# Weight block sums moved from GpSimd additions to accumulating DMAs, with three raw buffers in turn, in a kernel of attention and two expert layers

## The chip, the cores and the metric

One core of a Trainium2 chip runs the whole program in one launch. The metric is the device time in microseconds (us), median of several runs. Lower is better.

## The reference

Attention is computed for 2 batches, 8 heads, 768 positions and head size 64: a local window and 24 block summaries per head. Its output, 1536 tokens of 512 values, goes through two dense expert layers. All is float32.

```python
def _moe_ref(x, domain_probs, w1, w2):          # 4 experts, 512 -> 1024 -> 512
    p = domain_probs / (domain_probs.sum(-1, keepdims=True) + 1e-09)
    for e in range(E):
        h = np.maximum(x @ w1[e], 0.0)
        out += p[:, e:e + 1] * (h @ w2[e])
def _moe2_ref(x, w_gate, w1, w2):               # 8 experts
    P = np.exp(logits - logits.max())           # logits = x @ w_gate
    for _ in range(8):
        P /= P.sum(1, keepdims=True) + 1e-09
        P /= P.sum(0, keepdims=True) + 1e-09
        P *= N / E
    for e in range(E):
        out += P[:, e:e + 1] * (np.maximum(x @ w1[e], 0.0) @ w2[e])
```

## The kernel before

**Units and steps.** The two layers have 12 experts with 1024 hidden columns each. A unit is 256 hidden columns of one expert, so there are 48 units: 16 in the first layer, 32 in the second. The tokens form two blocks of 768. A step is one unit with one block: 96 steps. The border is the last step of the first layer, step 31.

**Seven products.** Both multiplications of a step are done on 2x2 blocks by a Strassen scheme of Winograd's form, with seven products instead of eight. The weights give the left operands: three raw blocks (`A11`, `A12`, `A22`) and four sums of blocks (`S1` to `S4`). The activations give the right operands: three raw blocks (`B11`, `B21`, `B22`) and four differences (`T1` to `T4`). Every operand is split into a high and a low float32r part (`hi`, `lo`), and three matmuls of 128x384 make one product of a 128 deep slice. A first product (`product`, L509, on `w1`) is six matmuls; a second product (L760, on `w2`) is three, and there are two rows of seven of them. A step is thus 42 + 42 matmuls.

**Weights (`add_weights`).** SP loads four raw 256-column blocks of `w1` or `w2` into a buffer `raw` (L641); each kind has one buffer of its own. ScalarE writes `hi` (L648) and the negated raw block into `lo` (L649). Then GpSimd issues a DMA that adds the raw block onto it (L652), which leaves the low part. This is done for a group of three raw blocks, then GpSimd forms the four sums in place with four `TENSOR_TENSOR` instructions (L659, `sums_of`), then two groups of two sums follow. The places for the raw-block groups are double, those for the sums are single: a new sum goes in only after the last matmul of the unit before has read the old one.

**Between the two multiplications.** ScalarE copies the first bank into others (`fork`, L684) so that products can accumulate; VectorE adds, applies ReLU times the row of expert weights (`relu`, L523), and forms the operands of the second multiplication (`add_hop`: `hi` on ScalarE L729, `lo` on VectorE L629). The second products are added to accumulators by VectorE (`evac`) or copied by ScalarE.

**The turn (`add_turn`).** At the border the accumulators of the first layer become the operands of the second: per block and half, seven additions on VectorE, seven `hi` on ScalarE, seven `lo`, of which VectorE makes four and GpSimd three. `add_gate` multiplies with `w_gate` on TensorE, `add_sinkhorn` does the eight normalisations in small VectorE instructions, and `plain` says in which units of the second layer's first expert ReLU is applied without the row, since it isn't there yet: all four. `add_scale` multiplies it in afterwards.

**The order.** All this is entered with `op` as a list of work with an engine, a cost (`SPAN`), its reads and writes and a due time. `run_work` plays the list through and writes each engine's instructions in the order that comes out. On the chip every engine and DMA queue runs its own list in that order. `FIRST`, `SECOND`, `HOP`, `GOFF`, `DCOFF`, `LEAD` and `LEAD2` set the due times.

Of the kernel before, what the change touches and what calls it, by code (L numbers as in the profile page):

```python
# [18 lines left out]
def local_global_attention_moe_moe(  # L19
# [92 lines left out]
    raw = {k: xp.tile([P, 4, FU], F32, name=f"raw{k}") for k in (1, 2)}  # L112
    quad = {n: xp.tile([P, HB], F32, name=n) for n in ("q11", "q12", "q21", "q22", "t2", "t4")}
# [4 lines left out]
    NU = len(units)  # L118
    KEYS = ("m1", "m2", "z", "c12", "c22")
# [20 lines left out]
    def loads(kind, u):  # L140
        layer, e, f = units[u]
        r = raw[kind]
        f0, f1, f2 = f * FU, f * FU + P, (f + 1) * FU
        if kind == 1:
            w = (w1a, w1b)[layer][e]
            h = DM // 2

            def part(c0, c1, a, z):
                return w[c0:c1, a:z].rearrange("(c p) f -> p c f", p=P)

            return [
                (r[:, 1:3].rearrange("x b (c f) -> x (b c) f", f=P), part(0, DM, f0, f1), (1, 2)),
                (r[:, 0].rearrange("x (c f) -> x c f", f=P), part(h, DM, f1, f2), (0,)),
                (r[:, 3].rearrange("x (c f) -> x c f", f=P), part(0, h, f1, f2), (3,)),
            ]
# [11 lines left out]
    def sums_of(kind):  # L167
        r = raw[kind]
        return (
            (0, ALU.add, 3, 0),  # L170
            (3, ALU.subtract, 1, 3),
            (1, ALU.subtract, 0, 1),
            (2, ALU.subtract, 2, 1),
        )

    def w_pieces(u, kind, hi_eng, lo_eng, sum_eng):
        r = raw[kind]
        hi, lo = wop[kind]
# [348 lines left out]

    def products(S, px, py, pz):
# [15 lines left out]
        vadd(q22, px, q22)  # L544
# [6 lines left out]
        product(S, A22, T4, px, False)  # L551
        relu(S, q21, px, 0)
# [74 lines left out]
    def lo_op(eng, out, src, hi, reads, writes, due, n=1):  # L627
        def fn(e=nc.gpsimd if eng == "POOL" else nc.vector):
            e.tensor_tensor(out=out, in0=src, in1=hi.bitcast(F32), op=ALU.subtract)  # L629

        span = ("p384", "p768")[n - 1] if eng == "POOL" else ("v", "v768")[n - 1]
        op(eng, span, reads, writes, due, fn, True)

    def add_weights(u, kind, start):
        r = raw[kind]
        hi, lo = wop[kind]
        R = [("raw", kind, i) for i in range(4)]
        for o, i, blocks in loads(kind, u):
            op(
                "SP", "ld", (), [R[x] for x in blocks], start,  # L640
                lambda o=o, i=i: nc.sync.dma_start(out=o, in_=i),  # L641
            )

        def group(s, n, b, key, due, span):
            src = r[:, b:b + n]
            h, l = hi[:, s:s + n], lo[:, s:s + n]
            rd = R[b:b + n]
# [3 lines left out]
                "POOL", "pd", rd, [key + ("lo",)], due + 0.05,  # L651
# [3 lines left out]
        group(slot(u, A22), 3, 0, wkey(kind, u, A22), start + 0.2, "a768")  # L655
        for o, f, x, y in sums_of(kind):
# [578 lines left out]
```

## Time and profile before

| | us |
|---|---|
| median of 3 runs (1613.19 to 1619.2) | 1614.82 |
| the profiled execution's own time | 1613.51 |
| its span in the profile | 1611.8 |
| TensorE busy in the span | 1541.8 (96%) |
| VectorE busy | 1393.4 (86%) |
| ScalarE busy | 1195.9 (74%) |
| GpSimd busy | 636.2 (39%) |

The span runs from the first to the last instruction of one execution. Busy TensorE time is not the same as full speed: matmuls overlap, and the clock that was granted is told apart in its own column. What counts is where TensorE sits idle, at which clock it runs, and whom it waits for.

### The profile page before, as it was taken

The page shows a single profiled execution, that of the slowest core. Times are in us where ns is not written, and L with a number is a line of the kernel's source. Part 1 is how long each engine was busy: PE and PEld are TensorE (multiplying, and loading weights), DVE is VectorE, ACT ScalarE, POOL GpSimd, SP SyncE. Part 2 cuts the span into 40 slices and gives each one's busy share as a digit, 9 for nine tenths or more (in the row PEclk, how much of TensorE's full clock was granted, in tenths as well). Part 3 has the DMA queues.
Part 4 walks back from the last instruction along what each step waited for, and adds up shares of the span by engine and source line. Part 5 has one row for each costly group of instructions (what it writes and reads, how often), then busy time and mean ns, then how long its engine had stood idle before and what let it go on. Part 6 is the DMA issues. An engine that isn't in the chain of part 4 may idle for free.

```text
span 1611.8 us, 26658 instructions
## 1 busy us (share of the span) xinstructions
PE 1541.8 (96%) x9098; PEld 1495.8 (93%) x9098; DVE 1393.4 (86%) x2694; ACT 1195.9 (74%) x2566; POOL 636.2 (39%) x753
## 2 busy tenths in 40 slices
PE   7888999999999988999999999999999999999998
PEld 6778999999999986998899999999999999999997
DVE  6877879988889997799998998888988988888988
ACT  5768777777778775866786877777776877777775
POOL 2864334334344344233333434334333433344330
PEclk9999999999999997999999999999999999999999
DMA  7823554554554542354354455544544554544542
GB/s 173 208 64 79 106 114 87 107 112 89 106 122 90 112 88 43 69 117 102 80 114 108 96 108 112 105 102 101 110 98 102 105 102 102 108 102 105 108 79 92
DMA packets 169241, 166.36 MB, mean 103 GB/s; under 512 B 44032, under 2 KB 128400, under 8 KB 169104
## 3 DMA queue, kind: packets, MB, share of 16 engines
q0 software_dynamic: 40608, 86.26, 30.9%
q1 hardware_dynamic: 128496, 78.39, 16.8%
q8 instruction: 71, 1.16, 0.3%
q14 instruction: 66, 0.54, 0.1%
HBM read 73.97 MB, written 3.22 MB: 48 GB/s over the span
## 4 chain that ended last, share of the span: by engine, by line
PE 61%; DVE 13%; DMA 12%; ACT 4%; issue 2%; POOL 0%; SPq 0%; ACTq 0%; DVEq 0%; POOLq 0%
PE bank L760 30%; PE bank L509 30%; DMA raw<-in_moe_w_dram 6%; DMA w1lo<-raw 5%; DVE h L629 4%; DVE q L523 2%; DVE t L133 1%; DVE z L130 1%; DVE c L130 1%; DMA w2lo<-raw 1%; DVE q L133 1%; DVE m L130 1%; ACT q L684 1%; ACT w1hi L648 1%; DVE q L130 1%
## 5 line engine op out<-in xcount | busy, mean ns | idle before, releaser
L760 PE MATMUL bank<-h,w2hi 128*128 128x384 f32 x2688 | 693.9, 338 | 13.0 <-ACT bank L771 4.6
L760 PEld LDWEIGHTS bank<-h,w2hi 128*128 128x128 f32 x2688 | 485.6, 189 | 26.9 <-DVE h L629 10.3
L509 PE MATMUL bank<-xhi,w1hi 128*128 128x384 f32 x1330 | 451.7, 340 | 19.3 <-ACT q L684 12.3
L509 PE MATMUL bank<-xhi,w1lo 128*128 128x384 f32 x1330 | 448.3, 337 | 2.5 <-DMA w1lo<-raw 2.5
L760 PE MATMUL bank<-h,w2lo 128*128 128x384 f32 x1344 | 450.6, 335 | 0.0
L509 PE MATMUL bank<-xlo,w1hi 128*128 128x384 f32 x1330 | 448.6, 337 | 2.0 <-DVE xlo L629 1.2
L659 POOL TENSOR_TENSOR raw<-raw 128x256 f32<-128x256 f32 x376 | 329.2, 876 | 298.3 <-issue 147.7
L629 DVE TENSOR_TENSOR h<-q,h 128x384 fp32r<-128x384 f32 x480 | 284.6, 603 | 9.2 <-ACT h L729 7.5
L771 ACT COPY bank<-bank 128x384 f32<-128x384 f32 x384 | 181.0, 471 | 143.3 <-PE bank L760 139.2
L509 PEld LDWEIGHTS bank<-xhi,w1hi 128*128 128x128 f32 x1330 | 251.9, 189 | 28.2 <-ACT q L684 19.1
L729 ACT CAST h<-q 128x384 fp32r<-128x384 f32 x480 | 241.9, 514 | 38.4 <-DVE q L133 19.6
L509 PEld LDWEIGHTS bank<-xlo,w1hi 128*128 128x128 f32 x1330 | 252.1, 190 | 3.9 <-DVE xlo L629 2.8
L509 PEld LDWEIGHTS bank<-xhi,w1lo 128*128 128x128 f32 x1330 | 252.1, 190 | 3.8 <-DMA w1lo<-raw 3.8
L760 PEld LDWEIGHTS bank<-h,w2lo 128*128 128x128 f32 x1344 | 253.4, 189 | 0.1
L652 POOL DMA_DIRECT2D w1lo<-raw x141 | 122.1, 866 | 317.9 <-PE bank L760 166.7
L652 POOL DMA_DIRECT2D w2lo<-raw x141 | 122.7, 870 | 254.5 <-ACT w2lo L649 158.3
L130 DVE TENSOR_TENSOR c<-bank,c 128x384 f32<-128x384 f32 x368 | 196.6, 551 | 4.7 <-PE bank L760 3.3
L130 DVE TENSOR_TENSOR q<-bank,q 128x384 f32<-128x384 f32 x190 | 105.3, 554 | 84.5 <-PE bank L509 81.7
L648 ACT CAST w1hi<-raw 128x768 fp32r<-128x768 f32 x141 | 97.9, 694 | 66.8 <-DMA raw<-in_moe_w_dram 42.5
L523 DVE SCALAR_TENSOR_TENSOR q<-bank,pb 128x384 f32<-128x384 f32 x174 | 96.3, 553 | 51.4 <-PE bank L509 47.4
L629 DVE TENSOR_TENSOR h<-t,h 128x384 fp32r<-128x384 f32 x192 | 120.8, 640 | 11.3 <-ACT h L729 10.4
L771 ACT COPY m<-bank 128x384 f32<-128x384 f32 x192 | 92.3, 481 | 41.1 <-PE bank L760 39.1
(177 smaller groups left out, 1809.9 us busy)
## 6 DMA issues: line engine op xcount, KB each, us to landing
raw<-in_moe_w_dram SPq DMA_DIRECT2D x96, 256.0 KB, 3.2
raw<-in_moe_w_dram SPq DMA_DIRECT2D x192, 128.0 KB, 3.1
w1lo<-raw POOLq DMA_DIRECT2D x94, 256.0 KB, 4.0
w2lo<-raw POOLq DMA_DIRECT2D x94, 256.0 KB, 3.3
w1lo<-raw POOLq DMA_DIRECT2D x47, 384.0 KB, 3.8
w2lo<-raw POOLq DMA_DIRECT2D x47, 384.0 KB, 4.8
pb<-prow SPq DMA_DIRECT2D x22, 384.0 KB, 3.8
vs<-in_v_dram SPq DMA_DIRECT2D x16, 240.0 KB, 4.3
```

The lines of the kernel that those rows point to most:

```text
L130: (eng or nc.vector).tensor_tensor(out=out, in0=x, in1=y, op=ALU.add)
L133: (eng or nc.vector).tensor_tensor(out=out, in0=x, in1=y, op=ALU.subtract)
L509: nc.tensor.matmul(pm, l[:, s, cs_], r[:, x, :], start=first and i == 0, stop=i == n - 1, skip_group_check=True,)
L523: nc.vector.scalar_tensor_tensor(out=out, in0=src, scalar=0.0, in1=PB[S[1]][:, th * HB:(th + 1) * HB], op0=ALU.max, op1=ALU.mult,)
L629: e.tensor_tensor(out=out, in0=src, in1=hi.bitcast(F32), op=ALU.subtract)
L648: aop(lambda: nc.scalar.copy(out=h, in_=src), rd, [key + ("hi",)], due, span)
L652: lambda: nc.gpsimd.dma_start(out=l, in_=src, accum_op=ALU.add),
L659: lambda o=o, f=f, x=x, y=y: nc.gpsimd.tensor_tensor(out=r[:, o], in0=r[:, x], in1=r[:, y], op=f),
L684: aop(lambda: nc.scalar.copy(out=out, in_=src), [kin], [kout], due)
L729: aop(lambda: nc.scalar.copy(out=hi, in_=q[name]), [name], [("hi", i)], due, "ah")
L760: nc.tensor.matmul(cut[bank], l[:, s, cols], hop[t][:, r], start=start and i == 0, stop=i == 2, skip_group_check=True,)
L771: aop(lambda: nc.scalar.copy(out=out, in_=src), [kin], [kout], due)
```

## The change

The sign variant: the `T` operands are renamed `N` and partly negated, so that every weight sum is an addition in place, in three operations of two, one and two blocks. GpSimd no longer adds them; it issues a DMA from raw block to raw block that accumulates. There are three raw buffers (the third is the attention's last output tile `xf`), used in turn by both kinds. The low parts of the turn and of `add_x` go to VectorE entirely. The rows of the second layer go into `PB`, plain units are three (`NPL`), and the planner's costs, product orders and due times have other values. The second gate half has 16 matmuls instead of 12. In attention, the first unit's sums are still made by GpSimd, in three instructions per kind, and VectorE negates one operand per x tile.

```diff
-    SLOT = {A22: 0, A11: 1, A12: 2, S1: 6, S2: 7, S4: 8, S3: 9}
+    SLOT = {A12: 0, A22: 1, A11: 2, S1: 6, S2: 7, S4: 8, S3: 9}
...
-    raw = {k: xp.tile([P, 4, FU], F32, name=f"raw{k}") for k in (1, 2)}
+    raws = [xp.tile([P, 4, FU], F32, name=f"raw{k}") for k in (1, 2)]
+
+    def turn_of(kind, u):
+        return (2 * (u - 1) + kind - 1) % 3 if u else kind - 1
...
-    def sums_of(kind):
-        r = raw[kind]
+    def sums_of(kind, u):
+        r = raw_of(kind, u)
         return (
-            (0, ALU.add, 3, 0),
-            (3, ALU.subtract, 1, 3),
-            (1, ALU.subtract, 0, 1),
-            (2, ALU.subtract, 2, 1),
-        )
+            (r[:, 0:2], r[:, 2:4], (0, 1), (2, 3)),
+            (r[:, 3], r[:, 2], (3,), (2,)),
+            (r[:, 0:3:2], r[:, 1:2].to_broadcast([P, 2, FU]), (0, 2), (1,)),
+        )
...
     def plain(S):
         layer, e, f = units[S[0]]
-        return layer == 1 and e == 0
+        return layer == 1 and e == 0 and f < NPL
...
-        "pd": (0.87, 4.2), "ld": (0.06, 3.2), "st": (0.06, 2.2),
+        "add1": (0.87, 4.0),
+        "add2": (0.87, 4.8), "add3": (0.87, 5.5), "ld": (0.06, 4.3), "st": (0.06, 2.2),
...
-        group(slot(u, A22), 3, 0, wkey(kind, u, A22), start + 0.2, "a768")
-        for o, f, x, y in sums_of(kind):
+        group(slot(u, A12), raws[i][:, 0:3], (0, 1, 2), wkey(kind, u, A12), start + 0.2, "a768")
+        for o, x, wr, rd in sums_of(kind, u):
             op(
-                "POOL", "p256", [R[x], R[y]], [R[o]], start + 0.5,
-                lambda o=o, f=f, x=x, y=y: nc.gpsimd.tensor_tensor(
-                    out=r[:, o], in0=r[:, x], in1=r[:, y], op=f
-                ),
-                True,
-            )
-        group(6, 2, 0, wkey(kind, u, S1), start + LEAD2, "a512")
-        group(8, 2, 2, wkey(kind, u, S4), start + LEAD2 + 0.1, "a512")
+                "POOL", f"add{len(wr)}", [R[j] for j in (*rd, *wr)], [R[j] for j in wr], start + 0.5,
+                lambda o=o, x=x: nc.gpsimd.dma_start(out=o, in_=x, accum_op=ALU.add),
+            )
+        group(6, *pair_of(kind, u, 0), wkey(kind, u, S1), start + LEAD2, "a512")
+        group(8, *pair_of(kind, u, 1), wkey(kind, u, S4), start + LEAD2 + 0.1, "a512")
...
-        for th, ops in ((0, ((B11, 0), (B21, 1))), (1, ((B11, 0), (T1, 0), (B22, 1)))):
+        for th, ops in ((0, ((B11, 0), (B21, 1))), (1, ((B11, 0), (N2, 0), (B22, 0), (B22, 1)))):
...
-    FIRST = {0: "1567324", 1: "1567342"}
-    SECOND = {0: "1256437", 1: "1524637"}
-    HOP, GOFF, DCOFF, LEAD, LEAD2 = 1.13, 0.16, 4.0, 1.0, 1.11
+    FIRST = {0: "1562734", 1: "1567342"}
+    SECOND = {0: "1526473", 1: "1526437"}
+    HOP, GOFF, DCOFF, LEAD, LEAD2 = 1.04, 0.16, 4.4, 1.0, 1.09
     LOPOOL = ()
+    LATER = {-2: 1.0, 1: -0.4, 2: -0.2, 3: 0.8}
+    SOONER = {-2: 0.6, -1: 0.2, 0: 0.2, 1: 0.6, 2: 1.0, 3: -0.2}
+    TURN = 0.8
```

**The order on GpSimd in the second layer.** Each engine runs its rows one after the other. Here is about one unit on GpSimd before; `raw_91` holds `w1`, `raw_92` holds `w2`, "waits" names semaphores of ScalarE, TensorE, SP's loads (`DMAHW`) and GpSimd's own DMAs (`DMASW`).

```order
L659 TENSOR_TENSOR raw_92<-raw_92 128x256 [waits DMASW4_49,Pool_49]
L659 TENSOR_TENSOR raw_92<-raw_92 128x256 [waits Pool_49] x2
L652 DMA w1lo<-raw_91 128x768 [waits DMAHW4_49,DMAHW7_49,PE_49,Activation_49]
L659 TENSOR_TENSOR raw_91<-raw_91 128x256 [waits DMAHW0_49,DMASW5_49,DMASW0_49]
L652 DMA w2lo<-raw_92 128x512 [waits PE_49,Activation_49]
L659 TENSOR_TENSOR raw_91<-raw_91 128x256 [waits DMASW7_49,Pool_49]
L659 TENSOR_TENSOR raw_91<-raw_91 128x256 [waits Pool_49]
L652 DMA w2lo<-raw_92 128x512 [waits Activation_49]
L659 TENSOR_TENSOR raw_91<-raw_91 128x256 [waits Pool_49]
L652 DMA w1lo<-raw_91 128x512 [waits PE_49,Activation_49]
L652 DMA w1lo<-raw_91 128x512 [waits PE_49,Activation_49,Pool_49]
L652 DMA w2lo<-raw_92 128x768 [waits DMAHW3_49,DMAHW2_49,Activation_49]
```

And one unit on GpSimd with the change; the twelve rows repeat with the three buffers in turn.

```order
L690 DMA raw_92<-raw_92 128x512 [waits DMASW4_49]
L690 DMA raw_92<-raw_92 128x256 [waits DMASW7_49]
L683 DMA w1lo<-xf 128x768 [waits DMAHW4_49,DMAHW5_49,DMASW1_49,DMAHW6_49,PE_49,Activation_49]
L690 DMA raw_92<-raw_92 128x2x256 [waits DMASW2_49,DMASW0_49]
L690 DMA xf<-xf 128x512 [waits DMAHW7_49,DMASW1_49]
L690 DMA xf<-xf 128x256 [waits DMASW3_49]
L683 DMA w2lo<-raw_92 128x512 [waits DMASW2_49,DMASW5_49,PE_49,Activation_49]
L683 DMA w2lo<-raw_92 128x2x256 [waits DMASW6_49,Activation_49]
L690 DMA xf<-xf 128x2x256 [waits DMASW4_49]
L683 DMA w2lo<-raw_91 128x768 [waits DMAHW1_49,DMAHW0_49,Activation_49]
L683 DMA w1lo<-xf 128x512 [waits DMASW7_49,PE_49,Activation_49]
L683 DMA w1lo<-xf 128x2x256 [waits Activation_49]
```

Each sum is now a DMA that waits for the landing of the sum before it, and the DMAs that make low parts stand between them on the same queue.

**The order on VectorE and GpSimd at the turn.** Before, GpSimd makes six of the first block's fourteen low parts (`xlo`).

```order
L629 TENSOR_TENSOR xlo_82<-c_00_1575,xhi_81 128x384
L652 DMA w2lo<-raw_92 128x768
L629 TENSOR_TENSOR xlo_82<-c_00_1577,xhi_81 128x384
L629 TENSOR_TENSOR xlo_82<-m_00_1571,xhi_81 128x384
L629 TENSOR_TENSOR xlo_84<-c_01_1576,xhi_83 128x384
L652 DMA w1lo<-raw_91 128x768
L629 TENSOR_TENSOR xlo_84<-c_01_1578,xhi_83 128x384
L629 TENSOR_TENSOR xlo_84<-m_01_1572,xhi_83 128x384
```

With the change all fourteen are on VectorE, between its other work; this is the densest piece.

```order
L652 SCALAR_TENSOR_TENSOR xlo_84<-z_1574,xhi_83 128x384
L657 TENSOR_TENSOR xlo_84<-c_01_1576,xhi_83 128x384
L144 TENSOR_TENSOR m_10_1579<-bank_1558,m_10_1579 128x384
L147 TENSOR_TENSOR c_01_1576<-c_01_1578,c_01_1576 128x384
L147 TENSOR_TENSOR q_94<-q_93,q_94 128x384
L652 SCALAR_TENSOR_TENSOR xlo_82<-m_00_1569,xhi_81 128x384
L657 TENSOR_TENSOR xlo_84<-c_01_1576,xhi_83 128x384
L652 SCALAR_TENSOR_TENSOR xlo_84<-m_01_1570,xhi_83 128x384
L657 TENSOR_TENSOR h_1565<-q_94,h_1565 128x384
L769 SCALAR_TENSOR_TENSOR t_97<-q_94,q_96 128x384
L652 SCALAR_TENSOR_TENSOR xlo_82<-c_00_1577,xhi_81 128x384
L652 SCALAR_TENSOR_TENSOR xlo_84<-c_01_1578,xhi_83 128x384
```

The low parts of the turn leave GpSimd and lengthen VectorE's list by six rows per block.

## Rows read from the trace of the kernel before

**Rows 1.** The page: busy time of each engine, share of the span, instructions.

```profile
PE 1541.8 (96%) x9098; PEld 1495.8 (93%) x9098; DVE 1393.4 (86%) x2694; ACT 1195.9 (74%) x2566; POOL 636.2 (39%) x753
```

**Rows 2.** Windows: us, busy PE, PEld, DVE, ACT, POOL, then clock, DMA share, GB/s.

```profile
160.00:560.00 400.00, 392.84 (x2232) 385.81 (x2231) 351.33 (x668) 304.81 (x640) 155.79 (x185) 1.00 0.50 104
560.00:800.00 240.00, 219.40 (x1182) 205.42 (x1181) 208.54 (x433) 171.87 (x368) 92.83 (x106) 0.95 0.40 85
800.00:1560.00 760.00, 749.77 (x4281) 742.60 (x4281) 667.32 (x1277) 584.10 (x1228) 297.90 (x355) 1.00 0.50 104
...
800.00:840.00 40.00, 40.00 (x232) 40.00 (x232) 35.82 (x71) 32.74 (x70) 13.99 (x18) 1.00 0.48 99
```

**Rows 3.** Waits of PE in 160 to 560 us: total us, times, longest.

```profile
PE bank L509 <- ACT q L684: 4.2, 6, 1.2
PE bank L509 <- DMA w1lo<-raw: 1.2, 2, 0.8
PE bank L760 <- DVE h L629: 0.6, 4, 0.2
```

**Rows 4.** Waits of PE in 800 to 1560 us.

```profile
PE bank L509 <- ACT q L684: 7.1, 9, 1.7
PE bank L509 <- DMA w1lo<-raw: 1.3, 2, 0.7
PE bank L760 <- DVE h L629: 1.1, 7, 0.2
```

**Rows 5.** Timeline of ACT near 1115 us, and of PE and SP there.

```profile
1116.01 0.83 ACT L648 CAST w1hi<-raw 128x768 fp32r<-128x768 f32 x1 [2.57 <-DMA raw<-in_moe_w_dram]
1116.75 0.47 ACT L684 COPY q<-bank 128x384 f32<-128x384 f32 x1
...
1117.66 0.44 PE L509 MATMUL bank<-xhi,w1hi 128*128 128x384 f32 x1 [1.50 <-ACT q L684]
...
1109.90 0.98 SPq L641 DMA_DIRECT2D raw<-in_moe_w_dram  x2
```

**Rows 6.** Waits of ACT on raw loads, whole span.

```profile
ACT w1hi L648 <- DMA raw<-in_moe_w_dram: 42.5, 29, 2.8
```

**Rows 7.** Windows around the turn, columns as in rows 2.

```profile
588.00:660.00 72.00, 59.42 (x276) 50.07 (x276) 57.66 (x94) 47.58 (x107) 29.60 (x31) 0.83 0.24 52
660.00:800.00 140.00, 131.98 (x746) 127.35 (x745) 125.99 (x290) 101.99 (x215) 51.51 (x61) 1.00 0.47 100
...
592.00:596.00 4.00, 1.84 (x10) 1.20 (x9) 4.00 (x6) 2.08 (x6) 2.36 (x3) 1.00 0.72 161
596.00:600.00 4.00, 1.74 (x4) 1.34 (x5) 3.97 (x6) 3.60 (x7) 2.88 (x4) 0.66 0.01 2
...
608.00:612.00 4.00, 3.77 (x12) 3.36 (x12) 4.00 (x7) 1.88 (x4) 1.35 (x2) 0.50 0.00 0
...
616.00:620.00 4.00, 4.00 (x25) 4.00 (x24) 3.17 (x7) 3.18 (x8) 0.15 (x1) 1.00 0.02 4
```

**Rows 8.** Groups of DVE by form, 560 to 800 us: busy us, mean ns.

```profile
L629 DVE TENSOR_TENSOR h<-q,h 128x384 fp32r<-128x384 f32 x64 | 37.1, 586 | 2.3 <-ACT h L729 2.1
L629 DVE TENSOR_TENSOR xlo<-z,xhi 128x384 fp32r<-128x384 f32 x8 | 8.0, 1026 | 1.5 <-ACT xhi L868 1.5
```

**Rows 9.** Groups of DVE by form, 1576 to 1612 us.

```profile
L629 DVE TENSOR_TENSOR h<-q,h 128x384 fp32r<-128x384 f32 x8 | 4.2, 551 | 0.0
```

**Rows 10.** Groups of POOL by form, 160 to 1560 us: the sums.

```profile
L659 POOL TENSOR_TENSOR raw<-raw 128x256 f32<-128x256 f32 x361 | 315.1, 873 | 291.5 <-issue 141.5 <-DMA w2lo<-raw 70.9 <-DMA w1lo<-raw 63.0
```

**Rows 11.** Line 652, GpSimd's accumulating DMAs: issue min/median/max ns; landing us.

```profile
L652 POOL DMA_DIRECT2D w1lo<-raw x141: 850/862/1016, 123.5 to 1557.2; - x141
L652 POOL DMA_DIRECT2D w2lo<-raw x141: 852/874/900, 127.9 to 1579.6; - x141
...
DMA to landing us min/median/max: 3.2/3.8/6.2
```

**Rows 12.** The page: GpSimd's DMA queue, packets, MB, share of 16 engines.

```profile
q0 software_dynamic: 40608, 86.26, 30.9%
```

More of the change, by code (lines that the diff above doesn't have):

```diff
@@ L205, in x_pieces @@
         yield split(hi[:, B11], lo[:, B11], b11, hi_eng, los[1])
-        yield sub(t1, b12, b11), sub(t2, b22, t1)
-        yield split(hi[:, T1:T3], lo[:, T1:T3], tx[:, :, HB:BLK], hi_eng, los[2])
-        yield sub(t3, t2, b11), sub(t4, b21, t2)
+        yield two(t1, b11, b12, ALU.subtract), two(t2, b22, t1, ALU.add)
+        two(t3, t2, b11, ALU.subtract)
+        two(t4, t2, b21, ALU.subtract)
+        yield sum_eng.tensor_scalar_mul(out=t2, in0=t2, scalar1=-1.0)
+        yield split(hi[:, N1:T3], lo[:, N1:T3], tx[:, :, HB:BLK], hi_eng, los[2])
         yield split(hi[:, T3:NOP], lo[:, T3:NOP], tx[:, :, 0:HB], hi_eng, los[3])
@@ L532, in products @@
         yield
-        product(S, S1, T1, py)
-        nc.scalar.copy(out=q22, in_=py)
+        product(S, S1, N1, py)
+        nc.scalar.mul(q22, py, -1.0)
         yield
-        product(S, S2, T2, px, False)
+        product(S, S2, N2, px, False)
         nc.scalar.copy(out=q12, in_=px)
@@ L681, in pr, with fork, gate, accu @@
             op("PE", "mm6", reads, [key], due, lambda: product(S, x, t, bank, first))
-        def fork(out, src, kin, kout, due):
-            aop(lambda: nc.scalar.copy(out=out, in_=src), [kin], [kout], due)
-        def gate(name, src, th, reads, due, two):
-            k = "ACT" if plain(S) else "DVE"
-            op(
-                k, "a" if plain(S) else "v", reads + [("pb", b)], [name], due,
-                lambda: relu(S, q[name], src, th), two and not plain(S),
-            )
-        def accu(name, bank, key, due):
-            vop(lambda: vadd(q[name], bank, q[name]), [key, name], [name], due, two=False)
+        def fork(out, src, kin, kout, due, by=1.0):
+            aop(lambda: nc.scalar.mul(out, src, by), [kin], [kout], due)
+        def gate(name, src, th, reads, due, two, neg=False):
+            if plain(S):
+                aop(lambda: relu(S, q[name], src, th, neg), reads, [name], due)
+            else:
+                vop(
+                    lambda: relu(S, q[name], src, th, neg), reads + [("pb", b)], [name], due,
+                    two=two,
+                )
+        def accu(f, name, bank, key, due):
+            vop(lambda: f(q[name], q[name], bank), [key, name], [name], due, two=False)
         for i, m in enumerate(FIRST[b]):
-            d = n + i / NOP
+            d = n + i / NOP + LATER.get(n - border, 0.0)
             e = d + 0.02
@@ L774, in evac @@
             t, key, bk = acc[b, k, dc], ("acc", b, k, dc), ("bank", bank)
-            if key in fresh:
+            if k == "c22" and n >= NS - 2:
+                vop(
+                    lambda: nc.vector.scalar_tensor_tensor(
+                        out=t, in0=cut[bank], scalar=-1.0, in1=t,
+                        op0=ALU.mult, op1=ALU.subtract,
+                    ),
+                    [bk, key], [key], due, two=False,
+                )
+            elif key in fresh:
                 fresh.remove(key)
@@ L788, in add_second @@
             cols = slice(dc * P, (dc + 1) * P)
-            d = n + 1 + GOFF + j / full
+            d = n + 1 + GOFF + j / full - SOONER.get(n - border, 0.0)
             e = d + 0.02
@@ L953, in tv, with pe @@
             vop(fn, reads, writes, due, "vs", False)
-        def pe(fn, reads, writes):
-            op("PE", "tr", reads, writes, due, fn)
+        def pe(fn, reads, writes, span="one"):
+            op("PE", span, reads, writes, due, fn)
         tv(
```

251 lines of the change are left out of this document (133 added, 118 removed), and 3 rows, old and new, of the table SPAN.

## The prediction

> **What bounds the kernel now.** I read the busy shares first. TensorE is busy 96% of the span, VectorE 86%, GpSimd 39% [rows 1]; so TensorE is the bound, and a change can only give back the time in which it sits idle or runs slowly. Where that is, the windows tell. At full rate it does 232 matmuls in 40 us, 0.172 us each [rows 2]; a step of 84 matmuls is 14.5 us, a unit of two steps 29.0 us. From 160 to 560 us it is idle 400 - 392.8 = 7.2 us, from 800 to 1560 us 760 - 749.8 = 10.2 us. Between them, around the border, 240 us hold 219.4 us of work at a mean clock of 0.95 [rows 2].
>
> In the two steady stretches the waits have names: ScalarE's copy of the first bank 4.2 + 7.1 = 11.3 us, a weight's low part 1.2 + 1.3 = 2.5 us, the hop's low part on VectorE 0.6 + 1.1 = 1.7 us [rows 3, 4]. The timeline shows what is behind the largest: SP issues a raw load at 1109.9 us, ScalarE stands 2.57 us at its conversion, behind it in ScalarE's list comes the copy, and TensorE loses 1.50 us [rows 5]. ScalarE has 29 such waits, 42.5 us, the longest 2.8 us [rows 6].
>
> At the turn TensorE does 276 matmuls in 588 to 660 us, which at full rate are 276 x 0.172 = 47.5 us: 24.5 us are lost. From 660 to 800 us it is 746 x 0.172 = 128.3 of 140 us: 11.7 us lost. VectorE works without a break from 592 to 600 us while TensorE does 14 matmuls; then the granted clock is at its lower level (0.50) until it is back at 1.00 from 616 us [rows 7].
>
> **The change part by part.** The sum is made against the profiled execution, 1613.5 us (span 1611.8); the median of the runs shown is 1614.8, 0.1% above it.
>
> *Sums by DMA and three buffers.* Per unit, eight additions of 0.873 us leave GpSimd [rows 10] and six DMAs come, issued at 0.86 us each [rows 11]. Their landing after that is not shown. GpSimd's present accumulating DMAs land in 3.2 to 6.2 us, median 3.8 [rows 11]. They use 30.9% of the DMA engines [rows 12] for 896 KB per kind and unit (128 x 768 and twice 128 x 512 values); the sums add 640 KB (128 x 512, 128 x 256 and 128 x 512), so 30.9 x 640/896 = 22%, and the share in the steady stretch goes from 0.50 [rows 2] to 0.72. I take 4.3 us for the landing, above the median because of that load; 3.2 and 6.2 are the ends.
>
> A buffer now serves again after 1.5 units instead of one: 14.5 us more. The three sums in it follow one another, so they take 3 x 4.3 = 12.9 us instead of 4 x 0.873 = 3.5: 9.4 us of the gift are spent, 5.1 are left. The longest wait of ScalarE on a load is 2.8 us, so a load should be there before its turn, and the 11.3 us go. What is late next is the low part of a sum: the DMA behind ScalarE's conversion. Before, it cost 2.5 us; with GpSimd's list holding waits on landings, I book the same again as new cost. The 1.7 us of VectorE's low part go as well: without additions on GpSimd that operation took 0.551 us at the end of the span, where GpSimd does nothing [rows 9], against 0.586 around the turn [rows 8]. Together 11.3 + 1.7 - 2.5 = **10.5 us**. The ends are 17.4 us (all idle time of both stretches) and, where GpSimd's list itself becomes the bound, a loss (below).
>
> *A rule on the shared ports.* The 282 accumulating DMAs are issued at 0.850 to 1.016 us, medians 0.862 and 0.874, beside a VectorE that is busy 86% of the span [rows 1, 11]: nothing shows that VectorE holds up the writing of descriptors. The Trainium skill (SBUF — State Buffer, "SBUF: two separate sides") warns of just this: a DMA issued from GpSimd starves while VectorE holds the pair of ports that they share, 620 ns alone against about 3100 ns behind a VectorE copy. By it the added sums would be the wrong trade; the last rival prices such landings from the rows, and I give it little.
>
> *The turn.* Six low parts per block move to VectorE: 12 x 0.551 = 6.6 us more [rows 9]. Its contested operations get shorter: the eight low parts on `z` alone by 8 x (1.026 - 0.551) = 3.8 us, the 64 of the hop by 64 x 0.035 = 2.2 [rows 8, 9]. So VectorE's work there stays about equal, and it remains the bound of the turn. By the new order, VectorE has 31 rows from the second low part of the first block to the last: 31 x 0.551 = 17.1 us. TensorE has 68 matmuls to do beside them, 11.7 us (second products of step 31 now stand between the first products of step 32). That leaves 5.4 us idle, twice for two blocks, and I let half of the 11.7 us behind 660 stay: 16.7 us lost instead of 36.2, a gain of 19.5. Eight more gate matmuls (2 x 4) cost 8 x 0.172 = 1.4. If an idle stretch of 5 us lowers the clock as the one at 592 did, some 14 us at 0.50 cost 7 us; I book half, 3.5. That leaves 14.6, and I take **14 us**. Ends: 5 us (VectorE's list as slow as now) and 28 us.
>
> The second layer's first expert has one plain unit fewer: eight more operations with the row on VectorE, 8 x 0.551 = 4.4 us, inside a stretch where it idles 240 - 208.5 = 31.5 us [rows 2]. I cost that at nothing; if the row were late, the unit's ReLU would wait on VectorE and hold up its whole list.
>
> *Attention and start.* GpSimd adds 1280 columns per kind instead of 1024, VectorE negates three tiles and makes three low parts more at the first step. Some of it is hidden. I book **-1 us**, with ends -4 and +3.
>
> Sum: 10.5 + 14 - 1 = 23.5 us, so 1613.5 - 23.5 = **1590 us**. By itself this case lies in 1578 to 1601.
>
> **The rivals.**
>
> *Only one half comes.* Either the sums land in 6 us: then 3 x 6.0 - 3.5 = 14.5 us eat the whole gift of the third buffer, loads are as late as before and the change doesn't do what it says for them, 1613.5 - 13 = 1600.5. Or the turn, where VectorE's work doesn't shrink, gives only its 5 us: 1613.5 - 14.5 = 1599. For the first speaks the higher DMA load, for the second rows 7.
>
> *Both fail.* 1613.5 - 5 + 1 = 1609.5, no change that can be told (0.5% is about what a measurement of this kernel can tell from none).
>
> *GpSimd's list becomes the bound: slower.* In the new order a sum stands behind the landing of the sum before it. Counted row by row, a unit passes five landings one after the other and two issues: 5L + 2 x 0.87 us. At 4.3 us this is 23.2 of 29.0 us. At L = (29.0 - 1.74)/5 = 5.45 us it is the whole unit, and from there each of the 47 units behind the first grows. At L = 5.8, halfway to the longest landing seen, a unit takes 30.7 us: 47 x 1.7 = 80 us, less the 13 of turn and start, 1613.5 + 67 = 1680 us. For it speaks that the longest landing, 6.2 us, was seen at a lower load; against it, the median.
>
> *Descriptors starve.* If all landings were as the longest, 6.2 us, a unit would take 32.7 us: 47 x 3.7 - 13 = 161 us, 1774 us. This is the mechanism of the Trainium skill's page above. The trace so far speaks against it.
>
> **How the numbers follow.** Forecast 0.52; one half 0.20; both fail 0.12; list on GpSimd 0.14; starving 0.02. Faster by over 0.5% (below 1606.7) are the first two: 0.72; same 0.12; slower 0.16. The range runs from 1576 to 1628: 0.05 is left out below and some 0.13 above, where only a small overrun of GpSimd's list is still inside.
>
> **What would show it.** Right: GpSimd's DMAs land in under 5 us though the DMA share is near 0.7; ScalarE's waits on raw loads shrink from 42.5 us to a few; TensorE's waits on ScalarE's copy nearly vanish between 160 and 560 and from 800 to 1560 us; the hop's low part takes 0.55 us everywhere; the stretch around the turn loses some 17 us instead of 36. Wrong: TensorE waits for weight low parts, a few tenths of a us or more in every unit, or for ScalarE behind a sum that hasn't landed; landings above 5.4 us; a clock at 0.50 for as long as before at the turn.

## The result and the profile after

The changed kernel takes 1575.26 us (median of 4 runs, 1572.66 to 1577.81), the kernel before, on the same chip, 1616.16 us: a ratio of 0.9747 [0.972, 0.9773], 40.9 us less. Forecast were 1590 us, 23.5 us less, and a range whose lower end, 1576 us, lies 0.7 us above the time. The direction and the likeliest case were right; the gain was undersized.

The page of the changed kernel, with the lines that answer to [rows 1] and [rows 12], and the accumulating DMAs of the sums (line L690; of a group: busy us, mean ns, idle before it; of an issue: KB, median us to landing):

```profile
PE 1522.5 (97%) x9106; PEld 1491.0 (95%) x9106; DVE 1320.0 (84%) x2716; ACT 1193.2 (76%) x2566; POOL 622.3 (40%) x642
...
q0 software_dynamic: 105280, 147.89, 55.8%
...
L690 POOL DMA_DIRECT2D raw<-raw x189 | 215.4, 1142 | 278.8 <-DMA raw<-raw 215.0
...
raw<-raw POOLq DMA_DIRECT2D x126, 256.0 KB, 4.3
```

VectorE is busy 73 us less with 22 instructions more. GpSimd's busy time barely moves: eight additions per unit have become six DMA issues of 1.1 us in the mean. The landing of 256 KB takes the 4.3 us that the prediction took.

Windows of the changed kernel, columns as in [rows 2] and [rows 7]:

```profile
160.00:560.00 400.00, 397.98 (x2292) 396.82 (x2291) 338.09 (x680) 310.08 (x653) 159.76 (x163) 1.00 0.77 150
560.00:800.00 240.00, 228.68 (x1283) 219.91 (x1283) 206.97 (x479) 183.86 (x395) 85.06 (x87) 0.98 0.69 132
800.00:1560.00 760.00, 757.19 (x4361) 753.45 (x4361) 649.71 (x1307) 586.84 (x1237) 295.53 (x299) 1.00 0.75 145
588.00:660.00 72.00, 69.98 (x395) 63.27 (x394) 55.56 (x136) 62.46 (x140) 22.29 (x23) 0.99 0.54 101
660.00:800.00 140.00, 133.56 (x756) 132.81 (x755) 125.49 (x290) 98.63 (x209) 50.59 (x52) 0.98 0.74 143
```

Count the matmuls instead of the idle time. A long stretch of the changed kernel in which TensorE hardly stands holds 1384 of them in 240 us, 0.1734 us each:

```profile
760.00:1000.00 240.00, 239.97 (x1384) 239.53 (x1383) 203.85 (x411) 187.84 (x395) 97.74 (x99) 1.00 0.79 153
```

What is lost in a window is its length less the matmuls times 0.1734. (The prediction's 0.172 is from a window of 40 us, where matmuls cut by its two ends weigh more; by it the two steady stretches before would have lost 39.8 us instead of 30.7. The differences hardly depend on it.)

| stretch, us | matmuls before, after | lost before, after | difference | idle before, after |
|---|---|---|---|---|
| 160 to 560 | 2232, 2292 | 13.0, 2.6 | 10.4 | 7.2, 2.0 |
| 560 to 800 | 1182, 1283 | 35.0, 17.5 | 17.5 | 20.6, 11.3 |
| 800 to 1560 | 4281, 4361 | 17.7, 3.8 | 13.9 | 10.2, 2.8 |

The three differences are 41.8 us, against 40.9 measured; start and end together gave about nothing. The two steady stretches gave 24.3 us, and the surroundings of the turn 17.5.

Waits of the changed kernel on the engines of [rows 3], [rows 4] and [rows 6] (us in total, times, longest). TensorE, 160 to 560 us:

```profile
PE bank L799 <- ACT bank L810: 2.0, 2, 1.5
```

TensorE, 800 to 1560 us:

```profile
PE bank L799 <- ACT bank L810: 1.9, 3, 1.3
PE bank L1097 <- DVE c L144: 0.8, 1, 0.8
```

ScalarE's conversions, 160 to 1560 us:

```profile
ACT w1hi L679 <- DMA raw<-raw: 12.8, 15, 2.1
...
ACT w1hi L679 <- DMA raw<-in_moe_w_dram: 0.9, 1, 0.9
```

In this window ScalarE's waits on raw loads have shrunk from 40.5 us to 0.9 (over the span they were 42.5 [rows 6]), and in their place stands the landing of a sum, 12.8 us. In the two steady stretches TensorE no longer waits for the first bank's copy behind it.

### The profile page after: what moved, and what is told of

Same layout as the page of the kernel before. It is cut to its first block, busy times and chain, and to the rows that moved or that the text cites. A ratio compares the mean times of both kernels' runs of the same rounds, so it can differ in the third digit from the quotient of the medians.

```text
span 1570.9 us, 26809 instructions
## 1 busy us (share of the span) xinstructions
PE 1522.5 (97%) x9106; PEld 1491.0 (95%) x9106; DVE 1320.0 (84%) x2716; ACT 1193.2 (76%) x2566; POOL 622.3 (40%) x642
## 4 chain that ended last, share of the span: by engine, by line
PE 84%; DVE 5%; DMA 4%; ACT 3%; issue 2%; POOL 1%; SPq 0%; ACTq 0%; DVEq 0%; POOLq 0%
PE bank L799 41%; PE bank L526 40%; DMA raw<-raw 2%; PE ps L397 1%; ACT h L662 1%; POOL xlo L141 0%; ACT bank L810 0%; DVE xfa L213 0%; ACT w2hi L679 0%; DVE z L144 0%; PE pv L356 0%; DVE h L657 0%; DVE q L543 0%; PE po L435 0%; PE bank L968 0%
## 5 line engine op out<-in xcount | busy, mean ns | idle before, releaser
L799 PE MATMUL bank<-h,w2hi 128*128 128x384 f32 x2688 | 688.9, 337 | 17.7 <-ACT bank L810 11.1
L799 PEld LDWEIGHTS bank<-h,w2hi 128*128 128x128 f32 x2688 | 483.6, 188 | 28.1 <-ACT bank L810 17.5
L526 PE MATMUL bank<-xhi,w1hi 128*128 128x384 f32 x1330 | 447.0, 336 | 1.8 <-ACT q L712 1.1
L662 ACT ACTIVATE h<-q 128x384 fp32r<-128x384 f32 x576 | 294.3, 521 | 73.4 <-PE bank L799 66.3
L690 POOL DMA_DIRECT2D raw<-raw x189 | 215.4, 1142 | 278.8 <-DMA raw<-raw 215.0
L810 ACT COPY bank<-bank 128x384 f32<-128x384 f32 x384 | 179.9, 469 | 127.8 <-PE bank L799 118.1
L657 DVE TENSOR_TENSOR h<-q,h 128x384 fp32r<-128x384 f32 x486 | 255.4, 549 | 5.6 <-ACT h L662 5.3
L144 DVE TENSOR_TENSOR c<-bank,c 128x384 f32<-128x384 f32 x364 | 200.6, 553 | 12.5 <-PE bank L799 8.2
L690 POOL DMA_DIRECT2D xf<-xf x93 | 104.3, 1122 | 152.5 <-DMA xf<-xf 115.8
L683 POOL DMA_DIRECT2D w2lo<-raw x96 | 96.8, 1015 | 170.6 <-ACT w2lo L680 109.1
L683 POOL DMA_DIRECT2D w1lo<-raw x93 | 94.6, 1021 | 127.3 <-PE bank L799 67.4
L810 ACT COPY m<-bank 128x384 f32<-128x384 f32 x196 | 93.5, 477 | 61.5 <-PE bank L799 57.6
L144 DVE TENSOR_TENSOR z<-bank,z 128x384 f32<-128x384 f32 x184 | 101.5, 552 | 22.2 <-PE bank L799 22.2
L144 DVE TENSOR_TENSOR m<-bank,m 128x384 f32<-128x384 f32 x188 | 103.4, 550 | 4.5 <-PE bank L799 4.4
```

Source lines behind the costliest of these rows:

```text
L144: (eng or nc.vector).tensor_tensor(out=out, in0=x, in1=y, op=ALU.add)
L526: nc.tensor.matmul(pm, l[:, s, cs_], r[:, x, :], start=first and i == 0, stop=i == n - 1, skip_group_check=True,)
L662: aop(lambda: nc.scalar.mul(out, src, -1.0 if neg else 1.0), reads, writes, due, "ah")
L683: lambda: nc.gpsimd.dma_start(out=l, in_=src, accum_op=ALU.add),
L690: lambda o=o, x=x: nc.gpsimd.dma_start(out=o, in_=x, accum_op=ALU.add),
L799: nc.tensor.matmul(cut[bank], l[:, s, cols], hop[t][:, r], start=start and i == 0, stop=i == 2, skip_group_check=True,)
```

## The experiments

Each kernel ran against the kernel before on one chip; the ratio to it stands with its 95% interval. All but three are combinations of five edits that undo a part of the change. A: the sums as GpSimd additions again, with an addition's costs in the planner; in the sign variant they are three operations over 1280 columns per kind and unit, where before there were four over 1024. T: two raw buffers.

```diff
-                lambda o=o, x=x: nc.gpsimd.dma_start(out=o, in_=x, accum_op=ALU.add),
+                lambda o=o, x=x: nc.gpsimd.tensor_tensor(out=o, in0=o, in1=x, op=ALU.add),
```

```diff
-        return (2 * (u - 1) + kind - 1) % 3 if u else kind - 1
+        return kind - 1
```

O: the product orders and due times of before. C: the costs of before for the DMAs. U: the due times of the turn empty.

```diff
-    FIRST = {0: "1562734", 1: "1567342"}
-    SECOND = {0: "1526473", 1: "1526437"}
-    HOP, GOFF, DCOFF, LEAD, LEAD2 = 1.04, 0.16, 4.4, 1.0, 1.09
+    FIRST = {0: "1567324", 1: "1567342"}
+    SECOND = {0: "1256437", 1: "1524637"}
+    HOP, GOFF, DCOFF, LEAD, LEAD2 = 1.13, 0.16, 4.0, 1.0, 1.11
```

```diff
-        "add1": (0.87, 4.0),
-        "add2": (0.87, 4.8), "add3": (0.87, 5.5), "ld": (0.06, 4.3), "st": (0.06, 2.2),
+        "add1": (0.87, 4.2),
+        "add2": (0.87, 4.2), "add3": (0.87, 4.2), "ld": (0.06, 3.2), "st": (0.06, 2.2),
```

```diff
-    LATER = {-2: 1.0, 1: -0.4, 2: -0.2, 3: 0.8}
-    SOONER = {-2: 0.6, -1: 0.2, 0: 0.2, 1: 0.6, 2: 1.0, 3: -0.2}
-    TURN = 0.8
+    LATER = {}
+    SOONER = {}
+    TURN = 0.5
```

The theory after the first look: the gain is the sums' departure from GpSimd's arithmetic, which slowed VectorE, and the third buffer is what pays for their landings. The rivals: the third buffer alone; the new orders and due times alone.

### One half at a time, with the new tables

**Edit A: additions, three buffers.**

> The changed kernel with its three sums made by GpSimd additions again (three buffers, orders and turn as changed). If the locked ports between GpSimd and VectorE cost most of the steady gain (24 us), VectorE's hop operation takes 0.60 us again and the time is near 1575 + 20 = 1595 us or above. If the third buffer is what counts, ScalarE still doesn't wait for raw loads and the time stays within 1575 to 1583 us. If the orders are what counts, the same: near 1575 us.

Measured: 1601.25 us, 0.9904 [0.9877, 0.9931]. **Edit T: DMA sums, two buffers.**

> The changed kernel with one raw buffer per kind, the sums still by DMA. If the third buffer counts: three landings of 4 us instead of 3.5 us of additions in a buffer that serves again after 29 us make loads some 8 us later than before; ScalarE waits for loads in most units and the time is 1600 us or more. If the locked ports or the orders count, it stays near 1575 to 1585 us.

Measured: 1785.41 us, 1.1043 [1.1008, 1.1078]. **Edits A and T.**

> Both undone: GpSimd additions and one raw buffer per kind, with the changed orders and turn. This is the weight path of before. If buffers and sums make the steady gain, it comes to 1575 + 24 = 1599 us. If the orders make it, 1575 to 1583 us.

Measured: 1686.60 us, 1.043 [1.0404, 1.0456]. So with these tables the sums by DMA are worth 26 us on top of three buffers, and cost 99 us without the third. Where the 26 us lie, the windows of edit A show:

```profile
160.00:560.00 400.00, 395.22 (x2263) 391.38 (x2262) 356.56 (x674) 311.30 (x649) 178.79 (x163) 1.00 0.50 106
560.00:800.00 240.00, 218.09 (x1181) 203.48 (x1181) 211.06 (x451) 171.85 (x368) 88.19 (x77) 0.96 0.40 83
800.00:1560.00 760.00, 752.97 (x4318) 747.71 (x4317) 677.43 (x1284) 589.19 (x1227) 335.40 (x306) 1.00 0.49 103
```

In the steady stretches 72 matmuls fewer than with the whole change (12.5 us), around the turn 102 fewer (17.7 us): 1181, as many as before the change. The waits of TensorE there, 160 to 1560 us, are led by VectorE and not by ScalarE:

```profile
PE bank L800 <- DVE m L144: 16.5, 20, 5.7
```

On VectorE the page shows the difference: the hop's low part takes 621 ns with the additions, 549 without. First edit A, then the whole change:

```profile
L657 DVE TENSOR_TENSOR h<-q,h 128x384 fp32r<-128x384 f32 x486 | 292.4, 621 | 5.9 <-ACT h L662 2.5
```

```profile
L657 DVE TENSOR_TENSOR h<-q,h 128x384 fp32r<-128x384 f32 x486 | 255.4, 549 | 5.6 <-ACT h L662 5.3
```

### The same four cases with the old tables

**Edits A, T, O, C and U**: of the change only the sign variant, the turn's low parts on VectorE, the gate's eight more matmuls and three plain units are left.

> The sign variant alone: GpSimd additions, one raw buffer per kind, and the turn, orders and DMA costs of before; only the signs, the low parts on VectorE, the gate's 8 more matmuls and three plain units stay. If the gain lies in buffers and sums, this takes the time of before, 1616 us, within 10. If the sign variant itself or the low parts on VectorE shorten something, below 1606 us. x3_pool_two took 1687 us with the DMA costs of the change: if that planner table, made for other landings, spoiled the order there, this is 70 us faster than it; if the two buffers with these sums are slow by themselves, it is near 1680 us.

Measured: 1614.74 us, 0.9991 [0.9976, 1.0006]. **A, O, C and U**: the third buffer comes.

> x8_all_old_costs (GpSimd additions, two buffers, old turn, orders and costs; 1615 us, the time of before) with one thing changed: three raw buffers in turn. If late loads behind ScalarE are what costs the steady stretches, 1615 - 11 = 1604 us or less. If GpSimd's additions beside VectorE hold the kernel anyway, 1610 to 1618 us.

Measured: 1627.73 us, 1.0065 [1.0039, 1.0091]. **T, O, C and U**: the DMA sums come.

> x8_all_old_costs with the other thing changed: sums by DMA, two buffers. Three landings of about 4 us stand where 3.5 us of additions stood, in a buffer that must serve again after 29 us: loads and sums come some 8 us later in every unit. If this chain binds, far slower than before, 1700 us or more (x2_two_raw: 1785 us). If the additions beside VectorE cost most, faster than 1615 us.

Measured: 1726.77 us, 1.0674 [1.064, 1.0707]. **O, C and U**: both come.

> The changed kernel with the old turn, orders and DMA costs together: of the change only sums by DMA, three buffers, signs and low parts on VectorE stay. If these two are the whole gain, 1575 to 1580 us. If the planner's DMA costs are needed as well, as x9_pool3_old_costs hints, 1590 us or more.

Measured: 1597.83 us, 0.989 [0.9856, 0.9924]. The medians side by side, in us:

| | two buffers | three buffers |
|---|---|---|
| old tables, additions | 1614.74 | 1627.73 |
| old tables, DMA sums | 1726.77 | 1597.83 |
| new tables, additions | 1686.60 | 1601.25 |
| new tables, DMA sums | 1785.41 | 1575.26 |

With the old tables neither half gains anything alone, and both together gain 17 us over the sign variant. With DMA sums in two buffers TensorE's longest wait is for low parts, and ScalarE waits for loads up to 5.0 us. The wait of TensorE in that kernel, 160 to 1560 us, and that of ScalarE:

```profile
PE bank L526 <- DMA w1lo<-raw: 29.5, 36, 2.3
```

```profile
ACT w1hi L679 <- DMA raw<-in_moe_w_dram: 27.8, 30, 5.0
```

What goes wrong with three buffers and additions is not the loads: ScalarE's waits on them sink from 24.8 us (two buffers) to 6.7, and the kernel is slower all the same. TensorE's longest sums there, 160 to 1560 us:

```profile
PE bank L800 <- DVE m L144: 13.5, 22, 1.2
PE bank L800 <- ACT bank L811: 13.2, 14, 1.4
```

VectorE and ScalarE are late with the accumulators, and which piece of the list makes them so isn't settled.

**Edits A and C**: additions, three buffers, new orders, old costs.

> GpSimd additions with three buffers and the changed orders and turn, with the DMA costs of before in the planner (3.2 us for a load, 4.2 for an accumulating DMA). If the planner's costs don't matter once there are three buffers, the 1601 us of x1_pool_sums. If they matter, some 10 us or more off that.

Measured: 1633.26 us, 1.0095 [1.0078, 1.0112], against 1601.25 with the new costs: additions in three buffers gain only with a list that suits them.

### Additions that nobody needs

The whole change, with four additions per kind and unit on a tile that nothing else uses:

```diff
+        for i_ in range(4):
+            op(
+                "POOL", "p256", [], [("idle", 0)], start + 0.5 + 0.1 * i_,
+                lambda: nc.gpsimd.tensor_tensor(out=idle, in0=idle, in1=idle, op=ALU.add),
+                True,
+            )
```

> The changed kernel with GpSimd additions put back for nothing: four per kind and unit of 128x256 on a tile of zeros that no one else reads, nothing depends on them. If additions on GpSimd slow VectorE's operations with two operands in SBUF and this is worth more than 10 us, VectorE's hop operation takes about 0.60 us again and the time is 1590 to 1605 us. If the gain lies in loads and their order alone, within 1575 to 1582 us.

Measured: 1632.84 us, 1.0096 [1.0063, 1.0128]. GpSimd had done the last of the 376 additions at 867 us, so one run shows both cases; up to there they stand about twice as densely as the sums before (376 in 741 us against 361 in 1400 [rows 10]). Windows of 80 us (columns as in [rows 2]), two with and two without them:

```profile
400.00:480.00 80.00, 79.00 (x447) 76.85 (x446) 74.52 (x135) 61.28 (x130) 60.97 (x74) 1.00 0.75 143
480.00:560.00 80.00, 77.62 (x435) 74.58 (x433) 75.27 (x130) 58.54 (x124) 60.41 (x74) 1.00 0.71 138
...
1040.00:1120.00 80.00, 80.00 (x464) 80.00 (x463) 67.78 (x136) 61.08 (x129) 32.22 (x33) 1.00 0.78 149
1120.00:1200.00 80.00, 80.00 (x462) 79.71 (x462) 68.43 (x139) 64.95 (x137) 33.74 (x34) 1.00 0.79 158
```

And the hop's low part on VectorE, with an addition to an accumulator that has one operand in a PSUM bank, first from 160 to 700 us, then from 800 to 1500 us:

```profile
L659 DVE TENSOR_TENSOR h<-q,h 128x384 fp32r<-128x384 f32 x169 | 133.4, 812 | 2.9 <-ACT h L664 2.1
L145 DVE TENSOR_TENSOR c<-bank,c 128x384 f32<-128x384 f32 x124 | 65.6, 547 | 2.7 <-PE bank L807 1.7
...
L659 DVE TENSOR_TENSOR h<-q,h 128x384 fp32r<-128x384 f32 x239 | 131.6, 575 | 1.4 <-ACT h L664 1.2
L145 DVE TENSOR_TENSOR c<-bank,c 128x384 f32<-128x384 f32 x190 | 104.7, 554 | 4.2 <-PE bank L807 2.0
```

With additions on a tile that VectorE never touches, the same instruction takes 812 ns instead of 575, and TensorE does 447 and 435 matmuls in 80 us instead of 464 and 462. The data can't be the cause, and neither can the place in the program: the whole change does 463 and 454 in the first two windows. The instruction with one operand in a bank takes 547 and 554 ns: it isn't slowed. The Trainium skill (SBUF — State Buffer, "SBUF: two separate sides") states such a rule: VectorE with two inputs from SBUF and GpSimd share a pair of ports, which whoever starts first holds for the whole instruction. By it the trace agrees: in the kernel before, the 72 low parts of the hop (behind 160 us) that began while a GpSimd `TENSOR_TENSOR` ran ended 0.42 us after it in the median.

An example from the kernel before, three additions on GpSimd and VectorE beside them:

```profile
964.97 2.91 POOL L659 TENSOR_TENSOR raw<-raw 128x256 f32<-128x256 f32 x3 [1.49 <-issue]
...
965.18 0.56 DVE L130 TENSOR_TENSOR m<-bank,m 128x384 f32<-128x384 f32 x1
965.66 1.63 DVE L629 TENSOR_TENSOR h<-q,h 128x384 fp32r<-128x384 f32 x2
```

The price before can be counted this way. From 160 to 1560 us, 169 `TENSOR_TENSOR` of VectorE with both inputs in SBUF began while GpSimd ran one: 879 ns in the mean, against 569 for the other 912. With an input in a bank it is 552 against 551. Against 0.55 us each, the 169 cost VectorE 56 us.

The additions that nobody needs also stand on the queue that issues the DMAs, so the 58 us between this kernel and the whole change are an upper bound for VectorE's part in it.

### The tables

**O.**

> The changed kernel with the product orders FIRST and SECOND and with HOP, DCOFF and LEAD2 of before. If the weight path makes the steady gain, within 1575 to 1583 us. If the orders make it, 1590 to 1600 us, with TensorE's waits in the steady stretches back.

**U.**

> The changed kernel without the shifts of due times around the border (LATER and SOONER empty, TURN 0.5 as before). With GpSimd additions in the changed order (x1_pool_sums) the stretch 560 to 800 us lost 36 us, as before the change. If the turn's gain of some 17 us comes from VectorE working without GpSimd additions beside it, this stays near 1575 to 1580 us. If it comes from the shifted due times, 1590 us or more.

**C.**

> The changed kernel with only the planner's DMA costs of before (3.2 us for a load, 4.2 us for every accumulating DMA, instead of 4.3 and 4.0 to 5.5). If these costs, which set the order of ScalarE's and GpSimd's lists, are what x14_both lacks, about 1595 us, with ScalarE waiting for raw loads again. If turn and orders are needed together, 1575 to 1580 us.

**O and C.**

> The changed kernel with old product orders and hop times, and old DMA costs in the planner; the turn as changed. If these two together make ScalarE reach loads too early, about 1590 to 1598 us, as x14_both. If their small losses only add up, 1575 + 2 + 4 = 1581 us.

**O and U.**

> The changed kernel with the old turn and old orders, with the changed DMA costs. If the losses add up, 1575 + 2 + 2 = 1579 us. If turn and orders lean on one another, 1585 us or more.

**C and U.**

> The changed kernel with the old turn and the old DMA costs. If the losses add up, 1575 + 2 + 4 = 1581 us. If turn and costs lean on one another, 1590 us or more.

| undone | us | ratio to before |
|---|---|---|
| nothing | 1575.26 | 0.9747 [0.972, 0.9773] |
| O | 1576.90 | 0.9751 [0.9729, 0.9774] |
| U | 1577.22 | 0.9757 [0.9738, 0.9775] |
| C | 1579.21 | 0.9764 [0.974, 0.9788] |
| O and U | 1579.32 | 0.977 [0.9749, 0.9792] |
| C and U | 1582.09 | 0.9786 [0.9763, 0.9808] |
| O and C | 1600.62 | 0.9906 [0.988, 0.9932] |

Undone by itself, none of the three tables can be told from the whole change. Orders and costs together are worth 25 us, and either of the two alone keeps nearly all of it. Without both, loads are late again; waits of ScalarE with O and C, 160 to 1560 us:

```profile
ACT w1hi L679 <- DMA raw<-in_moe_w_dram: 15.7, 10, 2.5
...
ACT w1hi L679 <- DMA xf<-in_moe_w_dram: 4.6, 3, 1.6
```

Which entry of the two tables does it is open.

### One plain unit more

```diff
-    NPL = 3
+    NPL = 4
```

> The changed kernel with four plain units as before (NPL 4). In the changed kernel VectorE waits 1.2 us for the row near 697 us, and TensorE then stands 3.8 and 2.7 us (705 and 726 us). If the row that is needed one unit earlier is behind these two waits, the time falls by 5 to 8 us to about 1569 us. If they come from VectorE's load at the turn alone, it stays at 1575 us.

Measured: 1572.52 us, 0.9724 [0.9705, 0.9742], the lowest of all, but not separate from the whole change. TensorE from 700 to 740 us (busy, clock, DMA share, GB/s), first with three plain units, then with four:

```profile
700.00:740.00 40.00, 33.55 (x176) 0.91 0.68 136
```

```profile
700.00:740.00 40.00, 37.47 (x213) 1.00 0.72 139
```

With three, VectorE waits 1.2 us for the row, and its list with the multiplications by the row (L150) holds up TensorE; waits of TensorE, 700 to 730 us:

```profile
PE bank L799 <- DVE m L144: 3.8, 1, 3.8
PE bank L799 <- ACT bank L810: 2.7, 1, 2.7
```

The fourth plain unit wins 37 matmuls here, 6.4 us, and most of it is lost in the 40 us behind, where it does 206 instead of 232. **The same with longer costs:**

```diff
-    NPL = 3
+    NPL = 4
...
-        "add1": (0.87, 4.0),
-        "add2": (0.87, 4.8), "add3": (0.87, 5.5), "ld": (0.06, 4.3), "st": (0.06, 2.2),
+        "add1": (0.87, 4.8),
+        "add2": (0.87, 5.4), "add3": (0.87, 6.2), "ld": (0.06, 5.0), "st": (0.06, 2.2),
```

> x6_npl4 (1572.5 us) with still longer DMA costs in the planner: 5.0 us for a load, 4.8, 5.4 and 6.2 us for accumulating DMAs. If it only matters that a list doesn't reach an operation before its data has landed, this is as fast or some us faster, 1566 to 1573 us, and ScalarE's waits on sums (some 17 us) shrink. If costs must fit the landings, or the chain of one buffer no longer fits into 1.5 units in the plan, slower: 1580 us or more.

Measured: 1601.33 us, 0.9904 [0.9874, 0.9935]. These longer costs lose 29 us against the same kernel without them (1601.33 less 1572.52), where the shorter ones of before (edit C) lose 4. Why they do is not shown.

## Why the prediction was wrong in size, point by point

**The steady stretches, +10.5 us: the step that failed.** Measured were 24.3 us, more than the end of 17.4, which the prediction called "all idle time of both stretches". The idle time was the wrong bound. The prediction counted the turn as matmuls at full rate, but sized the steady stretches from waits. Counted as the turn was, 30.7 us were lost there before (13.0 and 17.7), against 17.4 idle. Of the 24.3 us won, idle time makes 12.6 (17.4 less 4.8); the rest was won while TensorE counted as busy before and after. An end of 30.7 in place of 17.4 would have taken the measured gain in.

Why a wait costs more than the gap that it shows can be read from TensorE's timeline; before, at full rate:

```profile
689.15 0.33 PE L509 MATMUL bank<-xhi,w1hi 128*128 128x384 f32 x1
689.32 0.33 PE L509 MATMUL bank<-xlo,w1hi 128*128 128x384 f32 x1
689.49 0.33 PE L509 MATMUL bank<-xhi,w1lo 128*128 128x384 f32 x1
```

A matmul is recorded 0.33 us long, and the next one starts 0.17 us after it. A start that is late by less than 0.16 us leaves no gap, and a longer wait shows 0.16 us less than it costs. Start by start, the trace of before has 103 starts in the two stretches that are more than 0.02 us late. They cost 30.8 us, and the gaps show 17.4 of it. The weight loads in [rows 2] would have been the better bound: they stand idle 14.2 + 17.4 = 31.6 us.

The parts of the sum: the waits on the first bank's copy went from 11.3 us to none, as the load theory said; 3.9 us on another copy, that of the second products (L810), are left. Low parts as a new cost (-2.5) did not come: TensorE's idle time on them is 0.4 us over the span. VectorE's slowing by GpSimd's additions was booked at 1.7 us, the waits that carry its name. That was too little: in edit A the additions cost 72 steady matmuls, 12.5 us. Without the DMA sums, edit A does 68 steady matmuls more than the kernel before, 11.8 us, about what the prediction gave to the loads. (This is one order of undoing; with the old tables additions in three buffers gain nothing.) The whole list of VectorE was longer, 1393 us against 1320, and a wait names only the last instruction of a late list.

**Landing taken as 4.3 us:** right for 256 KB (4.3, on `xf` 4.1). The middle sum, 128 KB, lands in 2.6, so three in a row are shorter than the 12.9 us that were counted. DMA share 0.72 in the steady stretch: 0.77 and 0.75. That the sums need the third buffer holds: without it they cost 112 us with the old tables (1726.77 less 1614.74).

**The turn, +14 us:** 17.5 by the windows, well inside its ends of 5 and 28. "VectorE's work stays about equal" holds: 55.6 us busy between 588 and 660 against 57.7, but with 136 instructions instead of 94. The prediction had looked only at the low parts for what the additions cost. The contested rows were more than those; groups of VectorE before, 570 to 640 us:

```profile
L130 DVE TENSOR_TENSOR z<-z,m 128x384 f32<-128x384 f32 x4 | 4.5, 1115 | 0.0
...
L133 DVE TENSOR_TENSOR m<-c,c 128x384 f32<-128x384 f32 x4 | 3.7, 929 | 0.0
L130 DVE TENSOR_TENSOR m<-m,m 128x384 f32<-128x384 f32 x4 | 3.4, 854 | 0.0
```

And in the changed kernel, in the same window:

```profile
L144 DVE TENSOR_TENSOR m<-m,m 128x384 f32<-128x384 f32 x4 | 2.2, 547 | 0.0
...
L144 DVE TENSOR_TENSOR m<-c,c 128x384 f32<-128x384 f32 x4 | 2.1, 544 | 0.0
...
L144 DVE TENSOR_TENSOR z<-z,m 128x384 f32<-128x384 f32 x4 | 2.1, 544 | 0.0
```

The three groups come down from 1115, 929 and 854 ns to some 550. The gain had been put down to the new order alone, and that half of the step's reason failed. Matmuls in two pieces of the windows, 570 to 660 and 660 to 800 us: before 380 and 746; order without DMA sums (edit A) 437 and 689; DMA sums without the new tables (edits O, C and U) 437 and 742; both 472 and 756. In the first piece each brings 57 and both together 92, so a part of the gain comes from either; in the second, the additions cost edit A what it had won. (The planner made each list with other costs, so these aren't the same rows.)

The clock was booked at 3.5 us. Before, the granted clock was at its lower level (0.50) for 17.1 us from 597 us on and for 6.8 us from 628 us on. With the change it is there for 3.4 us from 586 us on, behind a wait of 1.7 us; TensorE's windows there (busy, clock, DMA share, GB/s):

```profile
584.00:588.00 4.00, 2.33 (x8) 0.74 0.99 237
588.00:592.00 4.00, 4.00 (x21) 0.83 0.46 84
```

It falls for as long twice more, at 705 and 726 us, in the two waits that are told of below. An estimate from these times: at half the rate the three cost at most 3 x 1.7 = 5.1 us.

**One plain unit fewer, "costed at nothing":** the warning given with it came true, a late row and waits of 3.8 and 2.7 us, at 705 and 726 us; undone, the gain is too small to be told.

**Attention and start, -1 us:** about 0.

**The rivals.** Only one half comes, or none: not so, the steady stretches and the turn both gained. GpSimd's list as the bound: it would have decided at landings of 5.45 us; the sums land in 2.5 to 8.4 us, median over all sizes 3.6 and for 256 KB 4.3, and TensorE hardly waits for low parts. Single landings above 5.4 us, which the prediction named as a sign of being wrong, did no harm that shows. Starving descriptors: the time that it gave, 1774 us, did not come. But the prediction stretched the rule that it used: the price is one behind VectorE copies, and of VectorE's 2694 instructions before 2473 were `TENSOR_TENSOR` and `SCALAR_TENSOR_TENSOR`, 44 were copies. So this kernel doesn't test it.

## What to carry to other kernels

Bound what a stretch can give back by the work that it did against the work at full rate, not by the idle time that its waits show. Two changes of which one pays for the other's latency have to be priced as a pair, and tried as a pair: with the old tables each alone made this kernel slower. Where GpSimd does arithmetic beside a busy VectorE, look through all of VectorE's groups for instructions of one form whose mean time differs, and price the difference on its whole list.

## What the runs showed that was not expected

An accumulating DMA takes GpSimd longer to issue: 862 and 874 ns median and at most 1016 before [rows 11], now for the sums on the raw buffers 908 ns median, 2133 at most, mean 1142. It isn't their number. By the sizes kept in the traces, DMAs with two pieces per partition (128x2x256) take 1.19 us or more in all kernels with the sign variant, also in edit A, which issues 282 as before; those with one piece have medians of 0.86 to 0.91 us. And a DMA that is issued close behind another has a longer record, which overlaps that of the other. GpSimd with the change, one piece and then twice two pieces, and edit A, one piece and two:

```profile
1007.15 0.86 POOL L683 DMA_DIRECT2D w2lo<-raw  x1 [2.01 <-PE bank L799]
1009.02 1.20 POOL L683 DMA_DIRECT2D w2lo<-raw  x1 [1.01 <-ACT w2lo L680]
1009.73 1.71 POOL L690 DMA_DIRECT2D raw<-raw  x1
...
1002.78 0.87 POOL L683 DMA_DIRECT2D w2lo<-raw  x1 [5.20 <-ACT h L662]
1004.06 1.20 POOL L683 DMA_DIRECT2D w2lo<-raw  x1 [0.41 <-ACT w2lo L680]
```

The records of the sums' issues add up to 320 us (215.4 on the raw buffers, 104.3 on `xf`), about as much as the additions did (329.2 over the span). The relief is not in GpSimd's time, but in that VectorE isn't slowed by it.

An accumulation from SBUF to SBUF was no burden on TensorE at DMA shares of 0.78 and 0.79: in the kernel with additions that nobody needs, the windows from 1040 to 1200 us are at full rate.
